# Two rounds of linear attention and gated ReGLU on one core: the second attention's queries of the first 1024 tokens by Strassen's seven products, in turns with the keys

## The chip, the cores and the metric

The kernel runs on one core of one Trainium2 chip. The core has a matmul engine (TensorE, PE in the profile, with its weight loads shown apart as PEld), a vector engine (VectorE, DVE), an activation engine (ScalarE, ACT), a general engine (GpSimd, POOL), and SyncE (SP), which here issues most of the transfers. On-chip data lies in SBUF; matmuls write their sums to PSUM banks, one bank being 128 partitions of 512 float32 numbers. The engines run side by side and wait for each other by semaphores.

The metric is the device time of one execution in microseconds, as the median of several runs. Times below are in microseconds (us) unless marked ns. A line number such as L457 is that of the kernel before.

## The reference

All inputs are bfloat16, and there is one sequence of 2048 tokens with 1024 features. Each layer is a residual step on a layer norm without gain or bias; attention and the gated layer are applied twice, with the same weights both times:

```python
def _A_ref(x, wqkv, wo):
    ...
    phi = lambda t: jnp.where(t > 0, t + 1, jnp.exp(t)) + 1e-6
    pq, pk = phi(q), phi(k)
    kv = jnp.einsum("bhsd,bhse->bhde", pk, v)
    z = jnp.einsum("bhsd->bhd", pk)
    num = jnp.einsum("bhqd,bhde->bhqe", pq, kv)
    den = jnp.einsum("bhqd,bhd->bhq", pq, z)[..., None] + 1e-6
    o = num / den
    ...

x = A_x
x = x + _A_ref(_layernorm(x, axis=-1), A_wqkv, A_wo)
x = x + _B_ref(_layernorm(x, axis=-1), B_W_gate, B_W_up, B_W_down)
x = x + _A_ref(_layernorm(x, axis=-1), A_wqkv, A_wo)
x = x + _B_ref(_layernorm(x, axis=-1), B_W_gate, B_W_up, B_W_down)
```

There are 32 heads of 32 features; `wqkv` is 1024 x 3072 (query, key and value columns), `wo` 1024 x 1024. `_B_ref` is `(relu(x @ W_gate) * (x @ W_up)) @ W_down` with 3584 hidden features. What the change touches is `q = layernorm(x) @ wqkv[:, 0:1024]` of the second attention, for tokens 0 to 1023, and the `phi` of it.

## The kernel before

**Tiles and layers.** The 2048 tokens are 16 tiles of 128 (x stays in SBUF as float32, `self.x[t]`), or four quarters of four tiles (`NQ` = 4, `QT` = 4). Layers 0 and 2 are the attentions (`layer_A`), layers 1 and 3 the gated layers (`layer_B`). "The second attention" is `layer_A` with l = 2; branches on `l` or `l == 0` tell the two apart.

**Seven products instead of eight.** Most of the matmuls are already done by Strassen's method in Winograd's form: with both operands cut into 2 x 2 blocks, four block sums of one operand (S1 to S4), four of the other (T1 to T4) and seven additions of products replace the eighth product. The gated layer does it in `glu` (matmuls at L939; PSUM tiles X, Y, Z and V per unit and weight) and in `down` (L1038), the attention in its keys-times-tokens products `m_products` (L541) and its outputs. Token sums S1 to S4 come from `sums_x` (L903; four DVE operations per 128 tokens, L912 to L915), weight sums from `make_gu` (L868) and `sums_d` (L888). The first gated layer makes the weight sums beside its products, and sends some of them to DRAM.

Only the projections of the attention to keys and queries (`project`, L457) are plain: one unit is one tile of 128 tokens times one half of the columns (512), eight matmuls of 128 x 128 by 128 x 512 into one PSUM bank. `k_unit` and `q_unit` then call `phi`: on ACT a relu of -x out of the bank (L403) and an exponential (L404), on DVE a join of both (L407), which reads the bank a second time and so frees it. Each finished key unit is also summed over tokens on POOL (`k_sum`, L476).

**Order of the second attention.** `run` calls its lists' units in turns, and after each unit advances the clock of `later` by one tick; `later.at(n, f)` calls f n ticks on. The units are: the eight key units of quarter 0 in turns with the eight query units of quarter 0, then key and query units of quarter 1 in turns, those of quarter 2, the keys of quarter 3. After that `m_products` begins; the queries of quarter 3 come later. In these units PSUM is four banks of `ps` plus, for every third unit, one of the two banks of `ps3` (`spare` in `project`). The `kvp` pool's two banks are free then. Within an engine's queue the order is that of the program as the scheduler emits it; engines run independently.

**Layer norm and transposes.** `ln_at` does one tile: statistics, one tick later the normalised tile, and `lag` ticks later the transpose into `xnT[l, q]` by a DMA on SP (`ln_turn`, L381). In the second attention, quarter 0 is normalised during the end of the first gated layer (`ln_later(l + 1, 0, 28, 6, 4)` in `layer_B`), while tiles 4 to 15 follow at ticks 2, 5, 8, ... of the attention's own units.

**Other work among the units.** The sums n1 to n3 of the normalised tokens and k1 to k3 of the keys (DVE, all through `op`, L508) for `m_products` are made as soon as both tiles of a pair, i and i + 8, are there, that is, from tile 8 on. The residual x of tiles 8 to 15 is sent to DRAM (`send_away`, L253, 512 KB each on SP), since its place serves for those sums.

**The weights' ring.** Weights are loaded through a ring of entries in the order of use (`_Ring`), at most five ahead in this stage (`depth`, and `free_before`); each takes one of 16 slots of 16 KB per partition (`big`), so that a load waits until the slot's old content has had its last reader. `plan_A` sets the order k0, k1, v0, q0, q1, v1, o0, o1 (two halves each of key, value, query and output weights, 1 MB each); SP issues the loads (L37).

Of the kernel before, what the change touches and what calls it, by code (L numbers as in the profile page):

```python
# [14 lines left out]
P = 128  # L15
NW = 512
HD = 32
QT = 4

# [70 lines left out]
class _Net:  # L90
    def __init__(self, tc, ctx, x_d, wqkv_d, wo_d, wg_d, wu_d, wd_d, out_d):
# [34 lines left out]
        self.td = self.spill.tile([P, self.U, 4, NW], F16, name="td")  # L126
        self.later = _Later()
# [293 lines left out]
    def plan_A(self, l):  # L421
        D = self.D
        cols = {"k0": D, "k1": D + NW, "v0": 2 * D, "v1": 2 * D + NW, "q0": 0, "q1": NW}
        for n in ("k0", "k1", "v0", "q0", "q1", "v1", "o0", "o1"):
            if n[0] == "o":
                c = NW * int(n[1])
                self.ring.add((l, n), self.wo_v[:, :, c:c + NW])
            else:
                self.ring.add((l, n), self.wqkv_v[:, :, cols[n]:cols[n] + NW])

    def layer_A(self, l, last_ln):
# [17 lines left out]
        def project(name, l_q, j, between=None):  # L449
            w = ring.get((l, name))  # L450

            spare = l_q < self.NQ - 1 and next(turns) % 3 == 2
# [158 lines left out]

        def z_chain(i):
            z_mult(*divmod(i, QT))
            if i < 10:
                later.at(2 + i % 2, lambda: z_chain(i + 1))
# [148 lines left out]
        if l == 0:  # L764
            steps = self.head()
        else:
            ring.free_before((l, "k0"))
        for i in range(QT, self.ST):
            self.ln_at((8 if l == 0 else 2) + 3 * (i - QT), l, i, 2)
            if l and i >= self.NS:  # L770
                later.at(4 + 3 * (i - QT), lambda i=i: self.send_away(i))
                later.at(10 + 3 * (i - QT), lambda i=i: sums(i - self.NS, n1, n2, n3))
# [10 lines left out]
        if l == 0:  # L783
            with self.tc.manual_schedule(engines={mybir.EngineType.DVE, mybir.EngineType.SP,
                                                  mybir.EngineType.Activation}):
                quarter0()
        else:
            run(first, column_major(q_unit, 0))
        for q in range(1, self.NQ - 1):
# [96 lines left out]
    def sums_d(self, t, u, ops=range(4)):  # L886

        T = t[:, :, :, :].bitcast(F16)  # L888
        for n in ops:
# [5 lines left out]
            if n == 3:  # L895
                self.later.at(2, lambda: self.nc.sync.dma_start(
                    out=self.td[:, u:u + 2, :, :], in_=T))

# [174 lines left out]
    def layer_B(self, l, final):  # L1073
# [6 lines left out]
        for c in range(2):  # L1080
# [3 lines left out]
            for u in range(self.U):  # L1084
# [3 lines left out]
                if first:  # L1088
# [6 lines left out]
                    if 3 < u < 12:  # L1095
                        self.later.at(4, lambda d=self.U - 4 + (u - 4) // 4 * 2, n=(u - 4) % 4: behind(
                            self.last_put, lambda: self.sums_d(wd[d], d, (n,))))
                if c == 0 and u == 1:
# [11 lines left out]
            elif not final:  # L1110
                self.ln_later(l + 1, 0, 28, 6, 4)
# [72 lines left out]
```

## Time and profile before

| what | value |
|---|---|
| median of 7 runs | 1467.32 us |
| lowest and highest of them | 1467.06 and 1467.76 us |
| the profiled execution | 1467.73 us |
| its span (first to last instruction) | 1465.9 us |
| granted clock of the matmul engine | 1.000 |
| matmuls at L457, both attentions | 1024, 223.7 us busy |
| transfers, whole span | 255.51 MB, mean 174 GB/s |

The span is counted from the first instruction to the last; the device's time is 1.8 us longer in the profiled execution. A matmul's busy time overlaps its neighbour's, since they are pipelined: 379 ns is listed for one at L457, while they follow each other more closely than that; the pace has to be read from a chain or a window. A releaser (`<-PE ps L457`) is what ended the idle time in front of an instruction.

### The profile page before, as it was taken

To read this page: it belongs to the slowest core of one execution; us is meant where nothing else is said; L and a number is where in the kernel's file an instruction comes from. 1 tells how busy PE (TensorE), PEld (TensorE's weight loads), DVE (VectorE), ACT (ScalarE), POOL (GpSimd) and SP (SyncE) were. 2 spreads that over 40 slices of the span, in tenths; PEclk is the share of its full clock that TensorE was granted. 3 is DMA by queue.
4 is the path that set the end of the run, shared out by engine and by line. 5 is a ranking of instruction groups with operands and counts; after the bars stand their busy time and mean duration, and the time that the engine had idled before them with its cause. 6 is when DMAs were issued, how large, how long until landed. Compare 5 with 4: busy or idle time off the path is not lost.

```text
span 1465.9 us, 18664 instructions
## 1 busy us (share of the span) xinstructions
PE 1457.1 (99%) x6920; PEld 662.9 (45%) x6959; DVE 842.9 (57%) x1484; ACT 577.3 (39%) x1027; POOL 285.8 (19%) x190
## 2 busy tenths in 40 slices
PE   9999999999999999999999999999999999999999
PEld 4444444444444444444444444444444444444444
DVE  6978698666684444455368665766435434333632
ACT  6772564333340333340067626633333203333200
POOL 1354851011100011110024476410110001111000
PEclk9999999999999999999999999999999999999999
DMA  9840787564559944446843029975444687444461
GB/s 283 235 157 8 181 219 203 186 219 162 204 172 255 345 153 143 145 137 192 254 100 73 1 33 279 255 236 175 144 144 151 187 257 247 147 144 151 149 203 43
DMA packets 318507, 255.51 MB, mean 174 GB/s; under 512 B 105808, under 2 KB 291536, under 8 KB 317520
## 3 DMA queue, kind: packets, MB, share of 16 engines
q1 hardware_dynamic: 307408, 233.01, 54.4%
q10 hardware_dynamic: 11008, 21.30, 3.9%
q8 instruction: 54, 0.88, 0.3%
q14 instruction: 37, 0.30, 0.1%
HBM read 195.04 MB, written 34.60 MB: 157 GB/s over the span
## 4 chain that ended last, share of the span: by engine, by line
PE 96%; DVE 2%; ACT 1%; issue 0%; DMA 0%; DVEq 0%
PE ps L457 15%; PE dy L1038 10%; PE yg L939 10%; PE yu L939 10%; PE dv L1038 7%; PE dx L1038 7%; PE xu L939 6%; PE xg L939 6%; PE ps L667 4%; PE zg L939 3%; PE zu L939 3%; PE vu L939 3%; PE vg L939 3%; PE my L541 3%; PE mv L541 2%; PE mx L541 2%
## 5 line engine op out<-in xcount | busy, mean ns | idle before, releaser
L939 PEld LDWEIGHTS <-w 128*128 128x128 f16 (+1 forms) x3136 | 306.7, 98 | 371.3 <-issue 1.4
L992 POOL TENSOR_TENSOR h<-m5u,m5g 128x512 f16<-128x512 f32 x56 | 71.9, 1285 | 810.0 <-DVE m5u L988 743.1
L457 PE MATMUL ps<-w,xnT 128*128 128x512 bf16 x1024 | 223.7, 379 | 0.2 <-ACT xnT L321 0.2
L1038 PEld LDWEIGHTS <-h 128*128 128x128 f16 x1120 | 109.6, 98 | 132.2
L457 PEld LDWEIGHTS <-xnT 128*128 128x128 bf16 x1024 | 99.3, 98 | 120.4 <-issue 1.7
L975 DVE TENSOR_TENSOR zg<-yg,m5g 128x512 f32<-128x512 f32 x56 | 39.1, 699 | 192.8 <-PE yg L939 192.8
L939 PE MATMUL yg<-s,w 128*128 128x512 f16 x448 | 115.0, 379 | 0.1
L939 PE MATMUL yu<-s,w 128*128 128x512 f16 x448 | 115.0, 379 | 0.0
L939 PE MATMUL xg<-xnT,w 128*128 128x512 f16 x448 | 115.0, 379 | 0.0
L939 PE MATMUL xu<-xnT,w 128*128 128x512 f16 x448 | 115.0, 379 | 0.0
L947 ACT ACTIVATE m5g<-m5g 128x512 f32<-128x512 f32 x56 | 35.2, 629 | 189.2 <-DVE m5g L988 185.3
L1038 PE MATMUL dy<-w,h 128*128 128x512 f16 x448 | 98.0, 379 | 0.0
L1038 PE MATMUL dx<-w,h 128*128 128x512 bf16 x436 | 96.7, 379 | 0.6
L404 ACT ACTIVATE e<-e,eps 128x512 f32<-128x512 f32 x128 | 92.4, 721 | 4.0
L403 ACT ACTIVATE e<-ps 128x512 f32<-128x512 f32 x128 | 75.6, 591 | 42.9 <-PE ps L457 41.8
L619 POOL TENSOR_TENSOR kvc<-pq,kvc 128x1024 f32<-128x1024 bf16 x32 | 73.6, 2301 | 61.7 <-DVE den L624 37.6
L667 PE MATMUL ps<-T,pqT 128*128 128x512 bf16 x374 | 83.0, 379 | 0.5
L956 ACT ACTIVATE m5g<-vg 128x512 f32<-128x512 f32 x56 | 33.4, 597 | 110.9 <-PE vg L939 85.2
L476 POOL TENSOR_TENSOR kvc<-kvc,slab 128x512 f32<-128x512 f32 x46 | 57.9, 1266 | 75.3 <-DVE slab L407 75.0
L950 DVE TENSOR_TENSOR h<-yu,r 128x512 f16<-128x512 f32 x56 | 38.7, 691 | 56.4 <-PE yu L939 56.4
L988 DVE TENSOR_TENSOR m5u<-yu,m5u 128x512 f32<-128x512 f32 x56 | 38.7, 691 | 52.0 <-PE yu L939 52.0
L1038 PEld LDWEIGHTS <-e 128*128 128x128 f16 x448 | 43.9, 98 | 52.8
(154 smaller groups left out, 1963.8 us busy)
## 6 DMA issues: line engine op xcount, KB each, us to landing
w<-in_B_W_gate_dram SPq DMA_DIRECT2D x56, 512.0 KB, 5.9
w<-in_B_W_up_dram SPq DMA_DIRECT2D x56, 512.0 KB, 5.4
w<-td SPq DMA_DIRECT2D x32, 896.0 KB, 4.7
w<-in_B_W_down_dram SPq DMA_DIRECT2D x24, 896.0 KB, 5.3
w<-tg SPq DMA_DIRECT2D x42, 512.0 KB, 7.0
w<-tu SPq DMA_DIRECT2D x42, 512.0 KB, 5.9
w<-in_A_wqkv_dram SPq DMA_DIRECT2D x9, 1024.0 KB, 7.1
away<-x SPq DMA_DIRECT2D x16, 512.0 KB, 4.1
```

Of the source, the lines that this page charges most:

```text
L403: nc.scalar.activation(out=e, in_=ps, func=ACT.Relu, scale=-1.0)
L404: nc.scalar.activation(out=e, in_=e, func=ACT.Exp, scale=-1.0, bias=self.eps6[:, 0:1])
L457: nc.tensor.matmul(by_row(ps), lhsT=self.xnT[l, l_q][:, kt, j * P:(j + 1) * P], rhs=w[:, kt, :].rearrange("p (b i d) -> p i b d", i=R, d=H ...
L476: nc.gpsimd.tensor_tensor(out=ksum[:, cols], in0=ksum[:, cols], in1=pk, op=ALU.add)
L541: nc.tensor.matmul(banks[j], lhsT=A(i)[:, j * P:(j + 1) * P], rhs=B(i), start=start and i == 0, stop=i == NS - 1, skip_group_check=True)
L619: nc.gpsimd.tensor_tensor(out=prod, in0=pq_of[sc, j], in1=zrow, op=ALU.mult)
L667: nc.tensor.matmul(ps, lhsT=pqT[sc][:, g, j * P:(j + 1) * P], rhs=T[g // 4][:, g % 4, n2 * NW:(n2 + 1) * NW], start=(g == 0), stop=(g == G ...
L939: nc.tensor.matmul(ps, lhsT=W[w][m][:, k, :], rhs=A[m][:, k, :], start=start and k == 0, stop=k == 3, skip_group_check=True)
L950: self.last_put = nc.vector.tensor_tensor(out=h[:, b, :], in0=ps, in1=R.pop(b), op=ALU.mult)
L975: self.last_z = nc.vector.tensor_tensor(out=Z[w], in0=Y[w], in1=V[w], op=ALU.add)
L992: nc.gpsimd.tensor_tensor(out=h[:, 3, :], in0=V["u"], in1=V["g"], op=ALU.mult)
L1038: nc.tensor.matmul(banks[j], lhsT=A(k)[:, j * P:(j + 1) * P], rhs=w[:, i, :], start=start and k == 0, stop=k == self.U - 1, skip_group_che ...
```

## The change

**Products.** In the second attention, the queries of quarters 0 and 1 (tokens 0 to 1023) are no longer made by `q_unit`. A new function `q_blocks` makes them as a 2 x 2 block product with seven products: the rows' blocks are quarter 0 and quarter 1, the inner blocks the two halves of the 1024 features, and the columns' blocks q0 and q1. Left blocks A1 to A7 are slices of the transposed tokens `xnT[l, 0]`, `xnT[l, 1]` and of their sums (`sums_x(l, 0, j)`, called in the first four ticks of this layer), right blocks B1 to B7 are slices of q0, q1 and of the weight sums t0, t1. A product of one tile pair j (tile j and tile 4 + j) is four matmuls of 128 x 128 by 128 x 512. Per pair:

- `one`: M1 into X (a `ps` bank), ACT copies X into Y (a `ps3` bank); M5 into V (a `kvp` bank), ACT copies it to SBUF (`qm5`).
- `two`: M2 onto X, `phi` of X (tile j, columns 0 to 511); M6 onto Y; DVE adds Z = Y + V into a `ps` bank.
- `three`: M7 onto Y; DVE adds V = Y + V in SBUF, `phi` of V (tile 4 + j, columns 512 to 1023); M3 onto Z, `phi` of Z (tile j, columns 512 to 1023).
- `four`: M4 onto Y, `phi` of Y (tile 4 + j, columns 0 to 511).

**Order.** The eight key units of quarter 0 now stand alone. Then, with key units of quarter 1 (and the first of quarter 2): `one` of pair 0; for every pair a key unit, `two`, a key unit, `three`, `one` of the next pair (after the last one a key unit), `four`. Afterwards the rest of the keys of quarter 2 in turns with its queries, and so on as before. For l = 2 `project` no longer takes `ps3` banks in the first two quarters.

**Weight sums.** The first gated layer, in its second half (chunk c = 1), loads both query halves again (`load_q` at unit 2, four loads of 512 KB), makes T1, T3, T2 and T4 in place (`sums_q`, one DVE subtraction of 128 x 2048 per unit, units 4 to 7, each put behind the last `put` of its unit), and stores them to two DRAM tiles `tq` of 1 MB. The ring loads them as entries t0 and t1.

**Layer norm and ring.** Quarter 1 is now normalised and transposed in the first gated layer's end as well, in steps of 3 ticks instead of 6. Tiles 8 to 15 follow at the ticks of `LN_AT`, their stores and sums at 2 and 8 ticks after each, as before. The ring's order in the second attention becomes k0, k1, q0, q1, t0, t1, v0, v1, o0, o1, and it is loaded up to t1 at the start.

The diff, without its blank lines and part of the unchanged surroundings:

```diff
 NW = 512
 HD = 32
 QT = 4
+LN_AT = (4, 8, 12, 16, 32, 35, 38, 41)
 
 
 class _Ring:
...
         self.tgu = {(w, u): self.spill.tile([P, 4, NW], F16, name=f"t{w}{u}")
                     for w in "gu" for u in range(self.U)}
         self.td = self.spill.tile([P, self.U, 4, NW], F16, name="td")
+        self.tq = [self.spill.tile([P, 8, NW], F16, name=f"tq{h}") for h in range(2)]
         self.later = _Later()
         self.phi_lag = 0
 
...
     def plan_A(self, l):
         D = self.D
         cols = {"k0": D, "k1": D + NW, "v0": 2 * D, "v1": 2 * D + NW, "q0": 0, "q1": NW}
-        for n in ("k0", "k1", "v0", "q0", "q1", "v1", "o0", "o1"):
-            if n[0] == "o":
+        for n in ("k0", "k1", "v0", "q0", "q1", "v1", "o0", "o1") if l == 0 else (
+                "k0", "k1", "q0", "q1", "t0", "t1", "v0", "v1", "o0", "o1"):
+            if n[0] == "t":
+                self.ring.add((l, n), lambda t, h=int(n[1]): self.nc.sync.dma_start(
+                    out=t[:, :, :].bitcast(F16), in_=self.tq[h]))
+            elif n[0] == "o":
                 c = NW * int(n[1])
                 self.ring.add((l, n), self.wo_v[:, :, c:c + NW])
             else:
...
         def project(name, l_q, j, between=None):
             w = ring.get((l, name))
 
-            spare = l_q < self.NQ - 1 and next(turns) % 3 == 2
+            spare = l_q < self.NQ - 1 and next(turns) % 3 == 2 and not (l and l_q < 2)
             ps = (self.ps3 if spare else self.ps).tile([P, NW], F32, tag="b" if spare else "a")
             for kt in range(KT):
                 if between and kt == KT - 2:
...
             if c == H - 1 and lag is not None:
                 later.at(lag, lambda: z_mult(sc, j))
 
+        def q_blocks():
+            xa, xb = self.xnT[l, 0], self.xnT[l, 1]
+            sa, sb = self.xs[l, 0]
+            q0, q1, t0, t1 = (ring.get((l, n)) for n in ("q0", "q1", "t0", "t1"))
+            t0, t1 = (t[:, :, :].bitcast(F16) for t in (t0, t1))
+            A = {1: xa[:, 0:4], 2: xa[:, 4:8], 3: sb[:, 4:8], 4: xb[:, 4:8], 5: sa[:, 0:4],
+                 6: sa[:, 4:8], 7: sb[:, 0:4]}
+            B = {1: q0[:, 0:4], 2: q0[:, 4:8], 3: q1[:, 4:8], 4: t1[:, 0:4], 5: t0[:, 0:4],
+                 6: t1[:, 4:8], 7: t0[:, 4:8]}
+            for sc in range(2):
+                a = self.slot(f"pq{l}_{sc}", [P, QT, D])
+                for i in range(QT):
+                    pq_of[sc, i] = a[:, i, :]
+            def steps(j):
+                S = {}
+                def mm(m, bank, start=False):
+                    for k in range(4):
+                        nc.tensor.matmul(by_row(bank), lhsT=A[m][:, k, j * P:(j + 1) * P],
+                                         rhs=B[m][:, k, :].rearrange("p (b i d) -> p i b d", i=R, d=HD),
+                                         start=start and k == 0, stop=k == 3, skip_group_check=True)
+                def one():
+                    S["X"] = self.ps.tile([P, NW], F32, tag="a", name=f"qx{j}")
+                    mm(1, S["X"], True)
+                    S["Y"] = self.ps3.tile([P, NW], F32, tag="b", name=f"qy{j}")
+                    nc.scalar.activation(out=S["Y"], in_=S["X"], func=ACT.Copy)
+                    v = self.kvp.tile([P, NW], F32, tag=f"kv{j % 2}", name=f"qv{j}")
+                    mm(5, v, True)
+                    S["V"] = self.temp(name="qm5")
+                    nc.scalar.activation(out=S["V"], in_=v, func=ACT.Copy)
+                def two():
+                    mm(2, S["X"])
+                    self.phi(S["X"], half(pq_of[0, j], 0))
+                    mm(6, S["Y"])
+                    S["Z"] = self.ps.tile([P, NW], F32, tag="a", name=f"qz{j}")
+                    nc.vector.tensor_tensor(out=S["Z"], in0=S["Y"], in1=S["V"], op=ALU.add)
+                def three():
+                    mm(7, S["Y"])
+                    nc.vector.tensor_tensor(out=S["V"], in0=S["Y"], in1=S["V"], op=ALU.add)
+                    self.phi(S["V"], half(pq_of[1, j], 1))
+                    mm(3, S["Z"])
+                    self.phi(S["Z"], half(pq_of[0, j], 1))
+                def four():
+                    mm(4, S["Y"])
+                    self.phi(S["Y"], half(pq_of[1, j], 0))
+                return one, two, three, four
+            return [steps(j) for j in range(QT)]
         def z_chain(i):
             z_mult(*divmod(i, QT))
             if i < 10:
...
         if l == 0:
             steps = self.head()
         else:
-            ring.free_before((l, "k0"))
-        for i in range(QT, self.ST):
-            self.ln_at((8 if l == 0 else 2) + 3 * (i - QT), l, i, 2)
-            if l and i >= self.NS:
-                later.at(4 + 3 * (i - QT), lambda i=i: self.send_away(i))
-                later.at(10 + 3 * (i - QT), lambda i=i: sums(i - self.NS, n1, n2, n3))
+            ring.load_to(ring.index((l, "t1")) + 1)
+            for j in range(QT):
+                later.at(1 + j, lambda j=j: self.sums_x(l, 0, j))
+        for i in range(QT if l == 0 else self.NS, self.ST):
+            at = 8 + 3 * (i - QT) if l == 0 else LN_AT[i - self.NS]
+            self.ln_at(at, l, i, 2)
+            if l:
+                later.at(at + 2, lambda i=i: self.send_away(i))
+                later.at(at + 8, lambda i=i: sums(i - self.NS, n1, n2, n3))
         if l == 0:
             first = self.head_units(lambda *a: k_unit(0, *a), lambda *a: q_unit(0, *a), *steps)
         else:
...
                                                   mybir.EngineType.Activation}):
                 quarter0()
         else:
-            run(first, column_major(q_unit, 0))
-        for q in range(1, self.NQ - 1):
+            run(first)
+            k = iter(row_major(k_unit, 1) + row_major(k_unit, 2)[:1])
+            Q = q_blocks()
+            todo = [Q[0][0]]
+            for j in range(QT):
+                todo += [next(k), Q[j][1], next(k), Q[j][2], Q[j + 1][0] if j + 1 < QT else next(k), Q[j][3]]
+            run(todo)
+            run(row_major(k_unit, 2)[1:], row_major(q_unit, 2))
+        for q in range(1, self.NQ - 1) if l == 0 else ():
             if (l, q) == (0, 1):
                 for i in range(self.U // 2 - 2):
                     later.at(1 + 8 * i, lambda i=i: self.make_d(2 * i))
...
             if n == 3:
                 self.later.at(2, lambda: self.nc.sync.dma_start(
                     out=self.td[:, u:u + 2, :, :], in_=T))
+    def load_q(self):
+        self.wq = [self.slot(f"wq{h}", [P, 2, 4, NW]) for h in range(2)]
+        for h, t in enumerate(self.wq):
+            for n in range(2):
+                self.nc.sync.dma_start(out=t[:, n, :, :], in_=self.wqkv_v[:, 4 * h:4 * h + 4, n * NW:(n + 1) * NW])
+    def sums_q(self, n):
+        (b11, b12), (b21, b22) = ([t[:, n, :, :] for n in range(2)] for t in self.wq)
+        f16 = lambda a: a.bitcast(F16)
+        out, a, b = ((f16(b11), b12, b11), (f16(b12), b22, b12), (f16(b22), b22, f16(b11)),
+                     (f16(b21), b21, f16(b22)))[n]
+        self.nc.vector.tensor_tensor(out=out, in0=a, in1=b, op=ALU.subtract)
+        if n % 2:
+            h = n // 2
+            self.later.at(2, lambda: self.nc.sync.dma_start(
+                out=self.tq[h], in_=self.wq[h][:, :, :, :].bitcast(F16).rearrange("p a k n -> p (a k) n")))
 
     def make_d(self, u):
         t = self.load_d(u)
...
                     if 3 < u < 12:
                         self.later.at(4, lambda d=self.U - 4 + (u - 4) // 4 * 2, n=(u - 4) % 4: behind(
                             self.last_put, lambda: self.sums_d(wd[d], d, (n,))))
+                if not final and c == 1:
+                    if u == 2:
+                        self.load_q()
+                    if 3 < u < 8:
+                        self.later.at(4, lambda n=u - 4: behind(self.last_put, lambda: self.sums_q(n)))
                 if c == 0 and u == 1:
                     for n, turn in enumerate(self.turns):
                         self.later.at(1 + n, turn)
...
             if c == 0:
                 self.ln_chunk(l, 1, 20, 3, 3, after)
             elif not final:
-                self.ln_later(l + 1, 0, 28, 6, 4)
+                self.ln_later(l + 1, 0, 28, 3, 4)
+                self.ln_later(l + 1, 1, 40, 3, 4)
             self.down(l, c, hT, final)
 
     def add_down(self, t, c, acc, final, last):
```

## The prediction

> **What bounds the kernel now.** I read the page's busy shares first, then its chain of waits, then that chain in order of time around the second attention, then that stage cut into windows, and last the order of instructions in it.
>
> ```profile
> PE 1457.1 (99%) x6920; PEld 662.9 (45%) x6959; DVE 842.9 (57%) x1484; ACT 577.3 (39%) x1027; POOL 285.8 (19%) x190
> ...
> PE 96%; DVE 2%; ACT 1%; issue 0%; DMA 0%; DVEq 0%
> ```
>
> The matmul engine is 99% of the span and 96% of the chain. That is an average; the chain in order of time (start us, us, what) says how it is in the stage that changes:
>
> ```profile
> 723.75 12.09 PE dy L1038 x56
> 735.84 96.69 PE ps L457 x448
> ```
>
> The projections of the second attention are one unbroken piece: 448 matmuls in 96.69 us, 215.8 ns each, with no other engine inside it. The stretch before it has the same pace (12.09/56 = 215.9). So here a matmul taken away is worth 215.8 ns, as long as nothing else makes PE wait. The windows (PE, PEld, DVE, ACT, POOL busy, clock, DMA share, GB/s) show who could:
>
> ```profile
> 759.00:768.50 9.50, 9.50 (x46) 4.29 (x45) 3.62 (x6) 7.26 (x11) 3.43 (x3) 1.00 0.00 1
> 768.50:778.00 9.50, 9.50 (x46) 4.32 (x45) 9.50 (x18) 7.61 (x14) 3.15 (x3) 1.00 0.63 112
> 735.70:832.50 96.80, 96.80 (x450) 43.90 (x449) 70.33 (x117) 73.37 (x118) 38.11 (x30) 1.00 0.27 57
> ```
>
> The clock is full. ACT is busy 7.3 to 7.6 us of each 9.5, and DVE 3.6 in one window but all 9.5 in the next, where the sums of normalised tokens and keys come in a batch. PE does not feel that batch now: a projection only needs a free bank, and up to six take turns.
>
> **The change part by part.** Three parts: fewer matmuls, a tighter order around them, and preparation elsewhere.
>
> Removed: 2 quarters x 4 tiles x 2 column halves x 8 = 128 matmuls at L457. Added: 7 products x 4 tiles x 4 = 112 of the same 128x512 size. Net 16 x 215.8 ns = **3.45 us** off the path. At L939 the same mix of f16 and bf16 operands runs at four matmuls in 0.86 us, so the pace holds. The Trainium skill ("TensorE: Matmul & The Clock Gate", Back-to-back issue gap) gives about 131 ns as the sustained spacing at 512 columns; by it the saving would be an estimated 2.1 us, but this trace shows 215.8 ns and decides.
>
> Added per turn (one tile pair of the four): two ACT copies, X to Y and M5 to V, and two DVE adds, Z = Y+V and V = Y+V. The 16 `phi` remain. These rows price them (timeline of before: ACT when it is behind, then DVE; then a copy and an add of the gated layer):
>
> ```profile
> 751.41 0.60 ACT L403 ACTIVATE e<-ps 128x512 f32<-128x512 f32 x1 [0.38 <-PE ps L457]
> 752.04 0.72 ACT L404 ACTIVATE e<-e,eps 128x512 f32<-128x512 f32 x1
> ...
> 781.17 0.72 ACT L404 ACTIVATE e<-e,eps 128x512 f32<-128x512 f32 x1
> 781.80 0.58 ACT L403 ACTIVATE e<-ps 128x512 f32<-128x512 f32 x1
> 782.41 0.72 ACT L404 ACTIVATE e<-e,eps 128x512 f32<-128x512 f32 x1
> 783.03 0.58 ACT L403 ACTIVATE e<-ps 128x512 f32<-128x512 f32 x1
> ...
> 511.48 0.70 DVE L975 TENSOR_TENSOR zg<-yg,m5g 128x512 f32<-128x512 f32 x1 [4.49 <-PE yg L939]
> ```
>
> A `phi` pair on a busy ACT takes 783.03-781.80 = 1.23 us, a copy (L962, 0.58) about 0.5, an add 0.70. A turn is 28 product matmuls and two key units, 44 x 0.2158 = 9.50 us of PE. ACT has six pairs and two copies, 6 x 1.23 + 1.0 = 8.4 us; it fits with 1.1 to spare. DVE has six joins (L407, one per 0.60) and two adds, 5.0 us, plus whatever of the batch falls in.
>
> What is new is that PE now waits for results inside a turn. In order: key unit, M2 onto X, M6 onto Y, key unit, M7 onto Y (needs Z = Y+V), M3, the next turn's M1 and M5, M4 onto Y (needs V = Y+V). And the next M2 and M6 need the copy of X into Y, which ACT does after both `phi` of this turn's V and Z. I follow the second turn, because in the changed program's order DVE has five 512-wide sums and two aggregates there between the join of X and the V add. On the clock of before: eight key units end at 735.67 + 64 x 0.2158 = 749.48; M1 and M5 take 1.73 and the first turn 9.50, so the second starts at 760.70. M6 ends 3.45 later, 764.15; M7, with three matmuls of the next M5 put ahead, at 760.70 + 6.04 + 0.65 = 767.4; M4 could start at 760.70 + 8.63 = 769.33. ACT sees a bank about 0.2 us after its last matmul was issued (737.60 against 735.67 + 1.73). The first turn's M7 ends at 751.21 + 6.04 + 0.43 = 757.68; plus 0.2 and an add, ACT starts on V and Z at 758.6: 2.2 for both `phi` in their interleaved order, 1.0 for two copies, 3 x 1.23 for M4, key and X, so the X pair ends near 765.6. DVE: the key join ends at 765.0, the Z add at 765.7 (needed at 766.5, M7's start), the join of X at 766.3, and the batch follows:
>
> ```profile
> L508 DVE TENSOR_TENSOR x<-x x15: 405/409/773, 746.0 to 792.5; 128x512 f16<-128x512 bf16 x15
> L508 DVE TENSOR_TENSOR x<-x,slab x7: 408/416/1378, 743.7 to 785.1; 128x512 f16<-128x512 bf16 x7
> L508 DVE TENSOR_TENSOR x<-x,x x7: 408/410/779, 745.7 to 786.7; 128x512 f16<-128x512 f16 x7
> ```
>
> (duration min/median/max.) Back to back they start 0.34 us apart (773.35 to 773.68 in the timeline), aggregates 0.12: 5 x 0.34 + 0.24 = 1.9, so the V add runs 768.2 to 768.9. M4's margin is 0.4 us. ACT then does relu, relu (0.48 apart), exp, exp (0.62) and the copy (0.58): 768.9 + 2.8 = 771.7; M2 could start at 760.70 + 9.50 + 1.73 = 771.93. Margin 0.2. Computed stall: **none**, by margins as small as the roundings. Bounds: below, zero; above, the batch with each kind once or twice at its maximum, 1.38 + 0.78 + 0.78 instead of three at 0.41, 1.7 us later, which costs M4 1.3 and M2 another 0.2 to 0.3, 1.6 in all. I take 0.2, near zero, since POOL's key sum (L476, 1.2 us) follows the key join, which ends at 765.0, and is over by 766.3 when the batch begins. The Trainium skill ("SBUF — State Buffer", Who interferes with whom) speaks against this: a DVE instruction with two SBUF inputs contends with a reading POOL instruction, and the loser blocks for all of it. The 1378 ns maximum agrees in size; if POOL did overlap, the estimate by that rule is one 1.2 us POOL sum in front of the V add, a stall of about 0.8, and 1464.7.
>
> The other turns have fewer sums ahead of the V add, three at most. The stage's start: the first key units have four banks, not six, and DVE now also does 16 sums of transposed tokens (L912 to L915, 0.42 us, 0.34 apart: 5.4 us), the first of them in its idle time before 731.3 (it waits 5.81 us for PE there). From 737.0, after the last add to x, to the end of the join that frees the bank of M1, DVE has two of these sums, five statistics and five joins (0.60 apart), two L170 (0.72 apart), six L508 (2.9 with two at 0.78) and two aggregates: 0.7 + 6.0 + 1.45 + 2.9 + 0.2 = 11.3, 748.3. M1 is due at 749.48: cover 1.2 us, beyond which each us late is a us lost. Cost taken: 0.
>
> Moved: the four transposes of quarter 1 go ahead of q0, q1 and all stores on SP's queue.
>
> ```profile
> 701.16 16.94 SPq L37 DMA_DIRECT2D w<-in_A_wqkv_dram  x5
> 719.97 17.41 SPq L253 DMA_DIRECT2D away<-x  x8
> 737.49 5.79 SPq L381 DMA_TRANSPOSE xnT<-x  x4
> ```
>
> Now they issue at 737.49. In the changed program the first waits only for the third-last product's first half, about 705.5, so they end issuing near 711.3 (5.79 us) and land by 715 (3.8 us). What they pass: q0 waits for a slot until about 711.5 anyway; the stores wait for results from 719.97 on. t0's and t1's loads wait for slots until about 723.6 and 729.6, land 7.1 us later, and are needed at 751 and 753.8. Hidden, with 17 us to spare. The stores of tiles 10 to 15 stand behind t0 and t1, but their x tiles are also finished only from 722 on. The later transposes wait for DVE and are needed 30 us after.
>
> First gated layer, second chunk: four 512 KB loads and two 1 MB stores more on SP, and four DVE differences of 128x2048, each twice an L873 (0.796), 1.6 us. Each stands after a unit's last product is put away and before the next Z sum, where DVE idles 4.49 us (the L975 row above). Hidden; without that cover 4 x 1.6 = 6.4. SP's issues are 0.4 us each and weights are loaded two units (24 us) ahead; 4 MB in 167 us adds 25 GB/s to 174.
>
> Sum: the profiled execution took 1467.73 (span 1465.9); 3.45 - 0.2 = 3.25 off gives span 1462.65. The median shown, 1467.32, is 0.41 lower than that execution; from it, **1464.1**.
>
> **The rivals.** (1) The V add is late: the margins of 0.4 and 0.2 us are used up in one or two turns. For it: DVE at 9.50 of 9.50 in a window today and L508 up to 1378 ns; against it: POOL's place. Stalls of 0.5 to 2.9 leave 1464.4 to 1466.8; with the 1.6 worked out, 1465.5. (2) Slower: the transposes of quarter 1 still land late, since SP is one queue. DVE's sums need them and stand in front of the last adds to x and of every `phi` join. If they landed where they would now, 743.3 + 3.8 = 747.1, the first join would end near 751.6 (five sums, three statistics and the last add come before it, 1.7 + 1.8 + 0.6, then its own 0.4), the fifth key unit, due at 742.6, would wait 9.0, and the result is 1467.32 + 9.0 - 3.45 = 1472.9. It decides from a landing after 738.1 (stall begins) and turns the sign after 741.5. Against it: 715. (3) The weight sums lose their cover and give back what the products save: 6.4 - 3.45, 1470.3; only the idle 4.49 us speak to it, and speak against.
>
> **How the numbers follow.** Forecast 60%, (1) 33%, (2) 4%, (3) 3%. 0.2% is 2.93 us, about what a measurement of this kernel can tell from no change, so faster means below 1464.39, a stall under 0.5: the forecast, 0.60. Rival (1) lies within: 0.33. The rest is slower: 0.07. The range starts at 1463.6 (no stall, 1463.87, less half of the runs' spread of 0.70) and goes to 1466.0, which takes in the upper bound of the stall, 1.6 to 1465.5, and most of (1).
>
> **What would show it.** In the changed profile the stage from the last `dy` to the first `mx` should be one piece of 432 matmuls, about 93.2 us, and the gated layer unchanged. A gap before M4 or M2 of the second turn, its releaser a DVE add or the ACT copy, shows (1); the first key units spread out, with DVE waiting for a transpose, (2); gaps in the second chunk, (3). The prediction is wrong if PE's pace in the turns is not 215.8 ns, or if DVE's or ACT's order costs a wait that I followed as hidden.

## The result and the profile after

| kernel | median, us | runs | lowest | span of the profiled execution |
|---|---|---|---|---|
| before | 1467.38 | 34 | 1466.98 | 1465.9 |
| changed | 1464.01 | 14 | 1463.74 | 1462.4 |

The changed kernel takes 0.9975 of the time of the one before, with a 95% interval from 0.9968 to 0.9982. That is 3.37 us less; the forecast was 1464.1, 3.2 less. One of the changed kernel's 14 runs took 5519.55 us, for a cause that nothing here shows; the ratio leaves it out.

In the chain of waits in order of time (start us, us, what), the one piece of 448 matmuls has become this:

```profile
735.62 13.81 PE ps L465 x64
749.44 0.86 PE qx L641 x4
750.30 0.86 PE qv L641 x4
751.16 1.73 PE ps L465 x8
752.89 0.03 issue
752.92 1.02 PE qx L641 x4
753.94 0.86 PE qy L641 x4
...
789.99 39.07 PE ps L465 x181
829.05 0.22 PE mx L549
```

From the first key matmul to the first `mx` it is 829.05 - 735.62 = 93.43 us, where it was 96.69. Sixteen matmuls at 215.8 ns would give 3.45; 3.26 came out. The missing 0.19 can be seen: 751.16 + 8 x 0.2158 = 752.89, and from there to 752.92 the chain has a pause; then the group of four M2 matmuls takes 1.02 instead of 0.86. In the timeline M1 of the first turn starts at 749.27, and M2 at 752.92, 0.19 later than eight key matmuls after 751.00 would allow. No other group of the stage starts late. (Below, a "gap" is always this: the start of a group of matmuls, less the start of the group before it, less its count times 0.2158.) The 0.22 us by which the stage starts earlier (735.62 against 735.84) are there from the first transfer of x on, in code that the change does not touch.

The same windows as before (PE, PEld, DVE, ACT, POOL busy, clock, DMA share, GB/s):

```profile
759.00:768.50 9.50, 9.50 (x46) 4.32 (x45) 8.23 (x19) 8.29 (x18) 2.32 (x2) 1.00 0.29 55
768.50:778.00 9.50, 9.50 (x46) 4.32 (x45) 6.42 (x11) 8.79 (x17) 2.37 (x2) 1.00 0.01 2
735.60:829.00 93.40, 93.37 (x434) 42.25 (x432) 77.09 (x132) 74.09 (x126) 37.36 (x30) 1.00 0.25 61
```

PE is as full as before at full clock. ACT's share of a turn rose to 8.3 to 8.8 of 9.5 (8.4 was worked out), and DVE has 77 us of work in 93 where it had 70 in 97.

(A slot of the weights' ring holds 8 KB per partition, 1 MB in all, not 16 KB as written further up; no step used it.)

### The profile page after: what moved, and what is told of

Its sections match the earlier page's. It is cut to its first block, busy times and chain, and to the rows that moved or that the text cites. A ratio compares the mean times of both kernels' runs of the same rounds, so it can differ in the third digit from the quotient of the medians.

```text
span 1462.4 us, 18678 instructions
## 1 busy us (share of the span) xinstructions
PE 1454.8 (99%) x6904; PEld 661.5 (45%) x6943; DVE 855.4 (58%) x1512; ACT 578.2 (40%) x1035; POOL 285.5 (20%) x190
## 4 chain that ended last, share of the span: by engine, by line
PE 96%; DVE 2%; ACT 1%; issue 0%; DMA 0%; DVEq 0%
PE ps L465 13%; PE dy L1132 10%; PE yg L1033 10%; PE yu L1033 10%; PE dv L1132 7%; PE dx L1132 7%; PE xg L1033 6%; PE xu L1033 6%; PE ps L732 4%; PE zg L1033 3%; PE zu L1033 3%; PE vu L1033 3%; PE vg L1033 3%; PE my L549 3%; PE mv L549 2%; PE mx L549 2%
## 5 line engine op out<-in xcount | busy, mean ns | idle before, releaser
L465 PE MATMUL ps<-w,xnT 128*128 128x512 bf16 x896 | 197.7, 379 | 0.2 <-ACT xnT L325 0.2
L465 PEld LDWEIGHTS <-xnT 128*128 128x128 bf16 x896 | 86.8, 98 | 105.3 <-issue 1.7
L407 ACT ACTIVATE e<-ps 128x512 f32<-128x512 f32 x112 | 66.1, 590 | 38.9 <-PE ps L465 38.1
```

The costliest lines, as they stand in the source:

```text
L407: nc.scalar.activation(out=e, in_=ps, func=ACT.Relu, scale=-1.0)
L465: nc.tensor.matmul(by_row(ps), lhsT=self.xnT[l, l_q][:, kt, j * P:(j + 1) * P], rhs=w[:, kt, :].rearrange("p (b i d) -> p i b d", i=R, d=H ...
```

## The experiments

All but e8_keys_too are the changed kernel with the edit shown; e8 changes more, as said there. Of longer edits the main lines are shown. "Before" ran beside each on the same chip and had a median of 1467.33 to 1467.52.

| run | median, us | ratio to before, 95% interval |
|---|---|---|
| e1_plain | 1467.38 | 1.0001, 0.9992 to 1.0010 |
| e2_no_ahead | 1466.02 | 0.9992, 0.9983 to 1.0000 |
| e3_late_q1 | 1466.81 | 0.9996, 0.9987 to 1.0005 |
| e4_two_adds | 1466.78 | 0.9998, 0.9989 to 1.0007 |
| e5_no_sums | 1464.00 | 0.9971, 0.9960 to 0.9983 |
| e6_copy_first | 1464.29 | 0.9977, 0.9967 to 0.9986 |
| e7_ln_spread | 1465.70 | 0.9985, 0.9976 to 0.9993 |
| e8_keys_too | 1468.58 | 1.0004, 0.9995 to 1.0012 |
| e9_ctl | 1464.50 | 0.9980, 0.9971 to 0.9989 |
| e9_own_turn | 1469.54 | 1.0018, 1.0009 to 1.0027 |
| a0_after | 1463.99 | 0.9978, 0.9969 to 0.9987 |
| e6_again | 1463.93 | 0.9975, 0.9966 to 0.9984 |

An interval is some 2.6 us wide from end to end, so differences between experiments rest on the gaps in their traces, which are set beside the medians. A trace shows one execution, and some of these lie above their medians: 1468.90 us for e4_two_adds, 1466.52 for e9_ctl, 1466.42 for e7_ln_spread (that of e8_keys_too, 1467.66, lies below). In the first three nearly the whole surplus comes before the stage, whose first key matmul starts at 737.27, 737.33 and 736.17 us instead of 735.46.

### Everything but the products: e1_plain

```diff
-                todo += [next(k), Q[j][1], next(k), Q[j][2], Q[j + 1][0] if j + 1 < QT else next(k), Q[j][3]]
+                a, b = [[lambda s=s, j=j, c=c: q_unit(s, j, c) for c in range(2)] for s in range(2)]
+                todo += [next(k), a[0], next(k), a[1], b[0], b[1]]
+            todo.append(next(k))
```

> All the preparation of the change stays (weight sums in the first gated layer, their stores and loads, token sums, quarter 1 normalised early, the new ring order and layer-norm ticks), but the queries of tiles 0 to 7 are again plain projections, 128 matmuls, in the same places between the keys; the third-unit use of the ps3 banks is back. Theory (the preparation is hidden, the gain is 16 matmuls of 215.8 ns): 1467.4 us, 1467.1 to 1467.8, and the projections of the second attention one piece of 448 matmuls in 96.7 us. Rival A (part of the gain comes from the moved layer norm or the new order): below 1466.5. Rival B (the preparation costs something that the products pay for): above 1468.0.

1467.38, and one piece of 448 matmuls from 735.43 to 832.12:

```profile
735.43 96.69 PE ps L465 x448
```

So weight sums, token sums, the added loads and stores, the moved layer norm and the new ring order cost nothing and bring nothing that can be measured; the 3.37 us are the products'. Rivals A and B fall. The prediction's third rival (weight sums without cover) falls with them.

### The order of the turns: e2_no_ahead, then e9_ctl and e9_own_turn

```diff
-            todo = [Q[0][0]]
+            todo = []
-                todo += [next(k), Q[j][1], next(k), Q[j][2], Q[j + 1][0] if j + 1 < QT else next(k), Q[j][3]]
+                todo += [next(k), Q[j][0], next(k), Q[j][1], Q[j][2], Q[j][3]]
+            todo.append(next(k))
```

> The seven products stay, but each turn is done in itself: key unit, M1 and M5, key unit, M2 and M6, M7 and M3, M4, with nothing of the next turn put between M6 and M7 or between M3 and M4. Theory (the order is what hides the vector engine's two adds): after the end of M2 the join of X is over 0.2 + 1.3 + 0.6 = 2.1 us later, the add Z = Y + V 0.7 later still, while M6 ends 0.86 after M2: M7 waits 1.9 us in each turn, M4 about 0.05. Four turns: 7.8 us, 1464.0 + 7.8 = 1471.8, range 1469 to 1474. Rival (PE does not feel the adds, as it does not feel the batch of sums): 1464.0, at most 1464.5.

It gave 1466.02, a quarter of the expected loss and neither theory's number. The timeline of PE in the first turn of e2 shows why:

```profile
755.20 1.03 PE L641 MATMUL qy<-w,s 128*128 128x512 f16 x4
756.07 0.59 PE L641 MATMUL qv<-w,s 128*128 128x512 f16 x2
756.50 0.81 PE L465 MATMUL ps<-w,xnT 128*128 128x512 bf16 x3
757.28 1.02 PE L641 MATMUL qy<-w,s 128*128 128x512 f16 x4
```

Between M6 (755.20) and M7 (757.28) stand two matmuls of the next turn's M5 and three of a key unit, which the program has behind M4: the scheduler, not the list in the program, sets the matrix engine's order, and it had filled the hole again. The run did not test what it was made for. It was done over with the matrix engine's order held to the program's, once with the changed kernel's list as a control (shown here) and once with the list of e2:

```diff
-            run(todo)
+            with self.tc.manual_schedule(engines={mybir.EngineType.PE}):
+                run(todo)
```

> The turns with the matrix engine's order held to the program's: key unit, M2, M6, key unit, M7, M3, the next M1 and M5, M4, where the scheduler of the changed kernel had moved a few matmuls of M5 ahead. A control for the next run. Theory: every add still has a key unit or the next M1 and M5 to hide it: 1464.0, 1463.8 to 1464.6.

> The order of e2 (each turn in itself, nothing between M6 and M7 or M3 and M4), now with the matrix engine's order held to the program's, so that no key matmul is moved in between again; only the fourth turn, whose followers lie outside, still gets six key matmuls there. Theory: the key's join ends 2.1 us after the key unit, the add Z then takes 0.7, and M7 could start 1.73 after it: M7 waits 1.05 us in three turns; M4 0.05 to 0.3, as the add V follows at once and M3 covers 0.86; the first M2 0.2. 3 x 1.2 = 3.5 us: 1467.5, range 1466.5 to 1469.0, so the whole gain of the products would be gone. Rival (the adds cost PE nothing even so): 1464.0 to 1464.6.

The control took 1464.50, with a gap of 0.20 before M2 of the first turn and one of 0.39 before M7 of the third. Each turn in itself took 1469.54, slower than the kernel before and above the expected range. In its timeline:

```profile
757.61 1.02 PE L641 MATMUL qy<-w,s 128*128 128x512 f16 x4 [1.05 <-DVE qz L660]
...
769.32 1.02 PE L641 MATMUL qy<-w,s 128*128 128x512 f16 x4 [1.98 <-DVE qz L660]
...
766.53 1.20 DVE L516 TENSOR_TENSOR x<-x,x 128x512 f16<-128x512 f16 x1
...
768.59 0.68 DVE L660 TENSOR_TENSOR qz<-qy,qm 128x512 f32<-128x512 f32 x1
```

M7 waits for the add Z, 1.05 us in the first turn, just as worked out, again 1.05 in the third, and 1.98 in the second, where the batch of sums (one of them 1.20 long) stands in front of the add; that batch the expectation had left out. The gaps of the stage sum to 5.2 us against 0.6 in the control. So the products in this order lose: what hides the adds is the foreign work between M6 and M7 and before M4, and at 5.04 us between the two medians this order is worth more than the 16 matmuls.

### The place of quarter 1's transposes: e3_late_q1

```diff
-            self.later.at(lag, lambda: self.ln_turn(layer, t, xn))
+            if layer == 2 and t // QT == 1:
+                self.pending.append(lambda: self.ln_turn(layer, t, xn))
+            else:
+                self.later.at(lag, lambda: self.ln_turn(layer, t, xn))
...
             ring.load_to(ring.index((l, "t1")) + 1)
+            for turn in self.pending:
+                turn()
```

> The four transposes of quarter 1 are issued behind the loads of q0, q1, t0 and t1 and four of the stores instead of ahead of them; all else stays. By the program's order SP issues them after t1's load (728.6 us in the changed kernel's trace) and the fourth store; the four take 5.8 to 9.0 us, so the last lands about 739 to 742. The vector engine has their sums in its queue ahead of the last adds to x and of every phi join. Theory (rival 2 of the prediction, and its threshold at a landing of 738.1): the first join comes 2 to 4.5 us later than its 739.0, PE waits nearly as long in the first key units, 1465.0 to 1468.5, about 1466.8, with the vector engine waiting for a transpose in front of a sum. If the place of the transposes does not matter: 1464.0.

1466.81: the size is right, the way to it not quite. The timeline of e3 (SP, then DVE):

```profile
728.36 6.64 SPq L386 DMA_TRANSPOSE xnT<-x  x4
...
733.37 0.43 DVE L1012 TENSOR_TENSOR s<-xnT 128x512 f16<-128x512 bf16 x1 [1.04 <-DMA xnT<-x]
...
739.86 0.69 DVE L415 SCALAR_TENSOR_TENSOR x<-ps,e 128x512 bf16<-128x512 f32 x1
...
750.25 0.67 DVE L415 SCALAR_TENSOR_TENSOR x<-ps,e 128x512 bf16<-128x512 f32 x1
```

DVE waits for the first transpose only (1.04 us). But its 16 sums begin at 733.37 instead of 728.97, and from then until 756 it is never idle. The first join comes only 0.86 us later than in the changed kernel (739.86 against 739.00), since part of DVE's other work now stands ahead of the sums or behind that join; the fifth comes 1.78 later (750.25 against 748.47). On the way three sums take 1.37 to 1.38 us (two of 1.37 in the changed kernel), so the growth from 0.86 to 1.78 is not all the transposes' own. PE's gaps are 0.73, 1.17 and 0.97, all between 748 and 756: a late start of the sums reaches PE although the landing never holds DVE up for more than 1.04 us, because DVE has no idle time left in which to make it good.

### More work in front of the add V: e4_two_adds

```diff
                     mm(7, S["Y"])
+                    for _ in range(2):
+                        d = self.temp(name="dd")
+                        nc.vector.tensor_tensor(out=d, in0=S["Y"], in1=S["V"], op=ALU.add)
```

> Two more adds Y + V (0.6 us each, result not used) stand in front of V = Y + V in each turn on the vector engine; nothing else changes. This measures the margins of M4 and of the next M2, read from the changed kernel's trace as 0.5 us (V add over at 768.8, M4 at 769.3) and 0.3 us (copy over at 771.6, M2 at 771.9) in the second turn. Theory: first turn, M4 just not late, next M2 late by 0.2; second turn, M4 late by 0.6 and M2 by 0.3; third turn between these; the fourth has no next M2: 1.5 to 2.0 us in all, 1465.7, range 1465.0 to 1466.5. Rival (the margins are wide, since PE has stalled nowhere in these turns): 1464.0 to 1464.4.

1466.78, above the range. The gaps are 0.21 before M2 of the first turn, 0.92 before M4 of the second (0.6 had been worked out), 0.30 and 0.43 before key units in the third, which wait for a bank, and 1.05 before M4 of the fourth. The next M2, for which 0.3 had been worked out, starts without a gap. What was left out is the fourth turn: it has no next M2, but its own M4. The timeline has both late M4, and the sum that stands in front of the add V of the second turn (PE, then DVE):

```profile
774.45 1.02 PE L641 MATMUL qy<-w,xnT 128*128 128x512 f16 x4 [0.76 <-DVE qm L667]
...
793.93 1.02 PE L641 MATMUL qy<-w,xnT 128*128 128x512 f16 x4 [0.89 <-DVE qm L667]
...
772.74 1.06 DVE L516 TENSOR_TENSOR x<-x 128x512 f16<-128x512 bf16 x1
```

It takes 1.06 us instead of 0.41, beside a GpSimd add of 772.36 to 773.52; in the fourth turn the sum there takes 1.07. The rival (wide margins) falls: 1.2 us more on DVE per turn cost 2.8 us in all. The edit did not leave all else as it was: the scheduler also moved key matmuls, seven ahead of M4 of the second turn and 13 instead of eight ahead of M4 of the fourth, into the time in which M4 waits.

### The batch of sums inside the turns: e7_ln_spread

```diff
-LN_AT = (4, 8, 12, 16, 32, 35, 38, 41)
+LN_AT = (14, 17, 20, 23, 26, 29, 32, 35)
```

> Tiles 8 to 15 are normalised at the ticks of the kernel before (14, 17, ... 35) instead of 4, 8, 12, 16 and 32 to 41; their stores and sums move with them. By the program's order no aggregate and no sum stands among the first eight joins any more, but four sums and scalings stand between the join of X and the add V in the second turn and three in the third. Theory: the wait of the activation engine (2.31 us) and the gap before M2 of the first turn go; the V add of the second turn comes 0.34 + 0.72 + 0.34 + 0.34 = 1.7 us after the join, as in the changed kernel (1.85): no new gap. 1463.8 to 1464.3. Rival (the batch must be over before the turns begin, as the changed ticks have it): gaps before M4 or M2 in the turns, or late transposes of quarter 2 before its first key unit, 1465 or more.

1465.70; the theory fell. The gap of the first turn is gone, as expected, but 0.38, 0.21, 0.26 and 0.76 appear in the later turns. The timeline in the third turn:

```profile
776.48 1.02 PE L641 MATMUL qy<-w,s 128*128 128x512 f16 x4 [0.22 <-DVE qz L660]
...
779.93 1.02 PE L641 MATMUL qy<-w,xnT 128*128 128x512 f16 x4
...
777.53 1.74 DVE L516 TENSOR_TENSOR x<-x 128x512 f16<-128x512 bf16 x3
779.20 0.68 DVE L664 TENSOR_TENSOR qm<-qy,qm 128x512 f32<-128x512 f32 x1
...
777.16 1.16 POOL L484 TENSOR_TENSOR kvc<-kvc,x 128x512 f32<-128x512 f32 x1 [5.99 <-DVE x L411]
```

Three sums, one of them beside a GpSimd sum, take 1.74 us instead of 1.0; the add V ends late and M4 (779.93) with it, by 0.21. ACT, which waits 1.63 us for that add, then passes the delay on to M2 of the fourth turn (0.26) and, by way of a join, to a key unit (0.76); the 0.38 is M7 of the third turn, for which the add Z is late:

```profile
779.91 0.63 ACT L407 ACTIVATE e<-qm 128x512 f32<-128x512 f32 x1 [1.63 <-DVE qm L664]
...
785.26 2.53 PE L465 MATMUL ps<-w,xnT 128*128 128x512 bf16 x11 [0.59 <-DVE pq L411]
```

So most of it is the prediction's first rival, the late add V. That 1464.01 to 1465.70 is near the 1.6 us worked out there as the upper bound is in part luck: that sum had 1.3 before M4 and 0.3 before M2 of one turn, and nothing for Z or for a key unit.

### The one gap that is left: e5_no_sums, e6_copy_first, and a0_after beside e6_again

The timeline of the changed kernel (DVE, ACT, POOL):

```profile
743.53 1.37 DVE L516 TENSOR_TENSOR x<-x,slab 128x512 f16<-128x512 bf16 x1
...
746.43 1.37 DVE L516 TENSOR_TENSOR x<-x 128x512 f16<-128x512 bf16 x1
747.73 0.27 DVE L165 BATCH_NORM_AGGREGATE mv<-stats 128x2 f32<-128x12 f32 x2
...
748.47 0.67 DVE L411 SCALAR_TENSOR_TENSOR x<-ps,e 128x512 bf16<-128x512 f32 x1
...
747.96 0.48 ACT L167 ACTIVATE rstd<-mv,eps 128x1 f32<-128x1 f32 x2 [2.31 <-DVE mv L165]
...
752.29 0.58 ACT L649 ACTIVATE qy<-qx 128x512 f32<-128x512 f32 x1
...
741.74 2.89 POOL L484 TENSOR_TENSOR kvc<-kvc,x 128x512 f32<-128x512 f32 x2 [1.38 <-DVE x L411]
746.32 1.20 POOL L484 TENSOR_TENSOR kvc<-kvc,x 128x512 f32<-128x512 f32 x1 [1.70 <-DVE x L411]
```

Two sums of 1.37 us lie beside GpSimd's adds, and each ends 0.27 to 0.28 us after the add beside it; the aggregate behind them is late, ACT stands 2.31 us at the two small operations that need it, with `phi` pairs queued behind, and copies M1 only at 752.29. M2, due at 752.73, waits for that copy.

```diff
-            later.at(1 + (10 if self.phi_lag else 0), lambda: k_sum(t, slice(c * NW, (c + 1) * NW)))
+            if not (l and 0 < t < QT):
+                later.at(1 + (10 if self.phi_lag else 0), lambda: k_sum(t, slice(c * NW, (c + 1) * NW)))
```

> The GpSimd sums of the keys of tiles 1 to 3 are left out in the second attention (so z lacks 384 tokens); all else stays. In the changed kernel's trace two of the five sums L516 between 742.9 and 747.8 take 1.37 us and one 0.71 instead of 0.41, beside GpSimd's adds; the aggregate after them comes at 747.7, the activation engine waits 2.31 us for it, is then behind, and copies M1 only at 752.8: that is the one gap of PE in the stage, 0.19 us before M2 of the first turn. Theory: without GpSimd's adds these sums take 0.41 to 0.43, the wait for the aggregate shrinks to under 0.5 and the gap is gone: 1463.8. Rival (the long ones have another cause): 1.37 and 2.31 stay, 1464.0.

The timeline of e5, without those GpSimd adds (DVE, ACT, PE):

```profile
743.34 0.42 DVE L517 TENSOR_TENSOR x<-x,slab 128x512 f16<-128x512 bf16 x1
...
745.28 0.42 DVE L517 TENSOR_TENSOR x<-x 128x512 f16<-128x512 bf16 x1
745.62 0.28 DVE L165 BATCH_NORM_AGGREGATE mv<-stats 128x2 f32<-128x12 f32 x2
...
745.86 0.48 ACT L167 ACTIVATE rstd<-mv,eps 128x1 f32<-128x1 f32 x2
...
751.12 1.89 PE L465 MATMUL ps<-w,xnT 128*128 128x512 bf16 x8
752.85 1.03 PE L642 MATMUL qx<-w,xnT 128*128 128x512 bf16 x4
```

All sums ahead of the aggregate are 0.41 to 0.42, ACT's wait is gone, and M2 starts 8 x 0.2158 after the key unit before it. The cause of the gap is shown. The median (1464.00 of 6 runs) does not show the 0.2 us.

```diff
-            run(first)
+            run(first[:-1])
...
-            todo = [Q[0][0]]
+            todo = [Q[0][0], first[-1]]
```

> M1 and M5 of the first turn are put ahead of the last key unit of quarter 0, nothing else. The copy of M1 then stands one phi pair earlier on the activation engine (1.24 us). Theory (the only gap left in the stage is M2 of the first turn waiting for that copy behind a backlog, 0.19 us): the gap is gone, 1463.8. Rival (the backlog itself is what is short, and the gap moves to the next unit that needs a bank): 1464.0 or more.

> The changed kernel as it is, on the same chip as the next run. 1464.0, and the one gap of 0.19 us before M2 of the first turn in its trace.

> The kernel of e6 (M1 and M5 of the first turn ahead of the last key unit of quarter 0) beside the changed kernel on one chip. Theory (its trace has no gap left in the stage): 0.2 us less than the run beside it, 1463.8. Rival (a gap of 0.19 us seen in one execution is not in the others): no difference.

In both traces of this edit the wait of ACT stays (2.3 us) and the gap is gone, while the changed kernel beside it has its 0.19 again: the gap needs both, ACT's backlog and a copy that stands behind it. Its medians, 1464.29 on one chip and 1463.93 beside 1463.99 on the other, are no measurable gain.

### Sixteen matmuls fewer still: e8_keys_too

The keys of quarters 0 and 1 are made by the same function, with weight sums of their own. The layer norm's ticks, the ring's order and the order of the turns change with it, so more than the keys' products is tried here. From the edit:

```diff
+            K = blocks("k", "s", lambda s, j: self.pk_home(l, s * QT + j), lambda s, j, c: later.at(
+                1, lambda: k_sum(s * QT + j, slice(c * NW, (c + 1) * NW))))
+            Q = blocks("q", "t", q_home, lambda *a: None)
+            turn = K + Q
```

> The keys of tiles 0 to 7 are made by the seven products as well, in four turns ahead of the queries' four, each turn's add covered by the next turn's M1 and M5; the weight sums of the keys are made in the first gated layer like those of the queries. Another 16 matmuls fewer, 3.45 us. The price: a key turn is 28 matmuls, 6.04 us of PE, and 4 x 1.23 + 2 x 0.5 = 5.9 us of the activation engine; the vector engine, which is busy without a gap from 729 to 750 in the changed kernel, has eight more adds. Theory: PE gets most of it, 0 to 2.4 us lost to late copies and adds: 1461.7, range 1460.6 to 1463.2. Rival (with 98% the activation engine becomes the bound of this stretch, or the vector engine's backlog does): 1463.5 to 1467.

1468.58: worse than the rival's range, and the theory fell. The stage has 7.5 us of gaps against 3.45 saved. A window of its key turns (columns as above), what PE waited for most in the stage (us in total, times, longest us), and two rows of the timeline (ACT, DVE):

```profile
749.00:762.00 13.00, 11.49 (x52) 5.03 (x52) 11.40 (x21) 10.79 (x23) 7.54 (x8) 1.00 0.61 115
```

```profile
PE ps L466 <- DVE pq L412: 2.2, 3, 1.4
PE kx L641 <- ACT ky L653: 2.0, 2, 1.1
PE qx L641 <- ACT qy L653: 1.0, 1, 1.0
```

```profile
756.75 0.58 ACT L653 ACTIVATE ky<-kx 128x512 f32<-128x512 f32 x1 [2.19 <-DVE x L412]
...
753.57 2.55 DVE L175 TENSOR_SCALAR slab<-x,mv,rstd 128x1024 bf16<-128x1024 f32 x2
```

PE is busy for 11.5 of 13.0 us, DVE for 11.4, ACT for 10.8. The rival named ACT or DVE's backlog as the bound; neither is full. ACT's copies into Y wait for the bank, which DVE's join frees (2.19 us in front of one of them), and just ahead of that join DVE spends 2.55 us on two scalings, while GpSimd is busy for 7.5 of the 13 us. That each engine hands its lateness on to the next, as every result passes from PE to ACT to DVE and back into the same banks, fits these waits, but no run separates it from the other changes.

## Why the prediction was right, step by step

- **16 matmuls at 215.8 ns, 3.45 us.** Right. The stage became 3.26 us shorter in the trace, 3.45 less one gap of 0.19, and e1_plain puts the products' worth at 1467.38 - 1464.01 = 3.37.
- **The second turn, "computed stall: none".** Right, to 0.2 us at each point. The timeline after (DVE, ACT, PE):

```profile
768.12 0.68 DVE L664 TENSOR_TENSOR qm<-qy,qm 128x512 f32<-128x512 f32 x1
...
771.07 0.58 ACT L649 ACTIVATE qy<-qx 128x512 f32<-128x512 f32 x1
...
769.32 1.03 PE L641 MATMUL qy<-w,xnT 128*128 128x512 f16 x4
...
771.91 1.03 PE L641 MATMUL qx<-w,xnT 128*128 128x512 bf16 x4
```

The add V starts at 768.1 (768.2 was worked out), the copy is over at about 771.6 (771.7), M4 starts at 769.3 and M2 at 771.9, both without a gap. That GpSimd's key sum would be over before the batch held there to 0.15 us (it ran from 765.27 to 766.43, the batch began at 766.28): the first sum took 0.43, and the long sums of the changed kernel lie elsewhere.
- **The 0.2 us taken for that stall.** The size is right, the place is not. The loss is in the first turn, and the step that failed is the stage's start: "cover 1.2 us, beyond which each us late is a us lost. Cost taken: 0." The join that frees M1's bank ended near 749.07 (748.47 and the 0.60 from join to join) instead of 748.3, and M1 starts, still on time, at 749.27: a cover of 0.2. Six L508 had been put at 2.9 us with two at 0.78; one took 0.71 and two 1.37. And only DVE was followed there: ACT, which waits 2.31 us for the aggregate in the same queue of sums, was not, and it is ACT's copy that M2 waited for. So one of the prediction's own signs of being wrong, a wait of ACT's that had been followed as hidden, did come, with 0.19 us. That it agreed with the 0.2 is luck.
- **GpSimd beside DVE.** The Trainium skill ("SBUF — State Buffer", Who interferes with whom) says that a DVE instruction with two SBUF inputs contends with a GpSimd instruction that reads SBUF, and that the lock is exclusive. The runs agree: 1.37 us beside GpSimd's adds, 0.41 to 0.42 without them (e5). The prediction weighed the rule at the second turn, where it did not bite, and not at the start, where it did.
- **The transposes and the loads of t0 and t1, "Hidden, with 17 us to spare".** Hidden, yes: in the changed trace the transposes are issued from 705.44 and take SP 9.05 us, not 5.79; the sums that need them begin at 728.97. The 17 us are those of t1: issued at 728.57, it lands some 8 us later, and M6 reads it at 753.78. Ahead of the sums DVE is idle for 3.65 us, which the profile puts down to the loads of t0 and t1; what holds the sums there, in front of a stretch in which DVE has no time to spare, was not tested. The rival's threshold (a landing after 738.1) was wrong: it was worked out for the first join, while the narrowest cover is at M1, 1.2 by the prediction's own sum and 0.2 in the trace. In e3 the sums wait for a transpose until 733.37, and that costs 2.8 us.
- **The weight sums, 1.6 us each in idle time of 4.49.** They take 1.22 (L987), and 3.35 to 3.36 us are left idle in front of the add Z. e1_plain: no cost that can be measured.
- **The rivals.** The late add V, held at 33%, does not occur with the changed ticks but with the old ones (e7: 1465.70) or with 1.2 us more work per turn (e4: 1466.78). So the margins were small, as said, and it was right to keep 1466 in the range. The transposes landed in time, and the weight sums kept their cover.

## What to carry to other kernels

Where a full matrix engine sets the time, as here, a product saved is worth its spacing in that stage, but only with foreign matmuls between each product and the next one that needs a result from another engine: in e9_own_turn the same 112 matmuls cost 5.2 us of waits without them. Follow every engine that stands in the loop (here DVE, then ACT by way of a two-column statistic) from the stage's start and not only at its densest point, and look for GpSimd instructions beside DVE's. Before an experiment that changes an order, see what order each engine really gets: in e2 the scheduler had put it back, and in e4 it had moved key matmuls into the hole that was to be measured.

## What the runs showed of the hardware

A sum of two 128x512 operands on DVE went from 0.41 to 1.37 us, more than three times as long, when a GpSimd add of 1.2 us ran beside it (e5 against the changed kernel). By way of the aggregate that became a wait of 2.31 us on ACT in front of an operation of 0.3 us on one column, and a relu whose bank PE had filled at about 746.0 started behind it only at 748.58.
